# A gated mix of sliding attention and a mish MLP: order of issue planned from measured durations, exponentials listed later, two chunks per bank in the half products

## The chip, the cores and the metric

The kernel runs on one core of a Trainium2 chip. The metric is the device time of one execution in microseconds (us); lower is better. Engines are named as the profile names them: PE (TensorE, its matmuls; PEld its weight loads), DVE (VectorE), ACT (ScalarE), POOL (GpSimd) and SP (SyncE, which here only issues DMAs).

## The reference

The input x has 2048 rows of 640 numbers. Two branches are mixed row by row with a gate, all in f32:

```python
def a_branch(x, wqkv, wo):          # 32 heads of 20, window of 8 keys, 2 rows apart
    q, k, v = heads(x @ wqkv)       # wqkv 640 x 1920
    idx = pos[:, None] - 2 * arange(8)[None, :]
    logits = einsum("bhsd,bhswd->bhsw", q, k[idx]) * 20 ** -0.5
    logits = where(idx >= 0, logits, -1e9)
    o = einsum("bhsw,bhswd->bhsd", softmax(logits), v[idx])
    return o.reshape(2048, 640) @ wo

def b_branch(x, w1, b1, w2):        # w1 640 x 1728, w2 1728 x 640
    h = x @ w1 + b1
    return (h * tanh(softplus(h))) @ w2          # mish

g = sigmoid((x * gate_w).sum(-1, keepdims=True))
out = g * a_branch(x) + (1 - g) * b_branch(x)
```

## The kernel before

**Matmuls.** Every f32 matrix product is made of three products of rounded parts (`mm3`, L349): each operand is split into a high part (an ACT copy, L317) and a low part (a subtraction, L320), and PE does high x high (L352), high x low (L353) and low x high (L354), mostly on 128 x 128 weights and 512 columns. The low part is marked "ANY" in many places: it may run on DVE or on POOL, and the planner below decides which.

**Attention.** The columns of wqkv are cut into four groups of heads (hq) and the rows into two halves (P); that gives eight units. For a unit, PE makes q, k and v (`qkv`), ACT evacuates the banks (L489, L491, L493), and `attention` does the rest for eight groups of 128 rows, in two sets of four: scores (DVE product L397 and sum L400), a small mask for the first rows on POOL (`bounded`, L407), the softmax (DVE maximum L413, which waits for the mask, subtraction L414, ACT exponential L415), the shares (DVE L419 to L422), and the weighted values (DVE product L428 and adds L432, L433, L435), turned by a DVE transpose (L360) and put into DRAM.

**First MLP product.** `mlp1` makes one 128 x 512 block of h for one of 13 full chunks of the 1728 features (fc) and one of four sets of 512 rows (tb), 15 matmuls each; ACT applies mish (L593) and, for some, a negated copy (L596). The weight chunks W1[fc] are loaded through one single buffer, `raw1`, and split (128 x 640). The last 64 features (`mlp1_rest`) come out of the columns of x @ w1 that were computed beside qkv: a DVE transpose of `hx`, a round trip through DRAM (h), and a mish on 64 rows.

**Second MLP product.** The product with w2 is done with seven half products in place of eight (a Strassen-like scheme): `a, b, c, e, g, d, f`, each over KH = 7 chunks of 128 features, with four or six banks of PSUM (p, q, u, w, r, v) at once. Its operands are the blocks 11, 21, 22 and sums of blocks t1 to t4, all in DRAM. `put` writes a block with an SP DMA, and `plus` (L586) adds onto one with an accumulate DMA that POOL issues. t2 and t4 are made of others:

```python
done[at("t2")] = t2 + [plus(at("t2"), lambda: blk[at("t1")][low], t2 + done[at("t1")], rows=n)]
done[at("t4")] = done[at("t4")] + [plus(at("t4"), lambda: blk[at("t2")][low], done[at("t4")] + done[at("t2")], rows=n)]
```

so the second accumulate reads what the first has written in DRAM and has to wait until that has landed. In `mlp2` the first chunk and the last chunk of each half product are done bank by bank (three matmuls for each bank), the five between them in two parts, one for each half of the rows. `after_product` frees the banks: ACT copies (L771), and sums with `two` (L775) on DVE or "ANY". At the end `wo_out` multiplies the attention's output with wo, adds (L915) and stores.

**The order of issue.** Nothing is scheduled while the kernel runs: the class `Plan` decides it when the kernel is built. Each piece of work is added as a task with an engine, an assumed time in ns, a rank and the tasks that it follows. `Plan.run` then walks through an imagined execution: whenever an engine is free it takes, of the tasks that are ready and whose buffers are free, the one with the lowest rank and number, and the instruction is emitted at that moment. The order on each engine is therefore a result of the assumed times. An end is told to tasks on other engines LAG ns later ("done") and to tasks on the same engine through a second event ("own"). SP's DMAs share one imagined wire (`size / 270.0` ns each); a `plus` of 128 rows carries a size of 128 x 7000, so its imagined landing is some 3.3 us after its issue. Rings hold the buffers (8 banks, 7 `raw`, 3 `w`, 4 `hb`, one `raw1`); `ANY` work goes to DVE while DVE does scores only once it has been ready for PATIENCE = 2000 ns, and POOL keeps quiet beside the scores.

PE's own order is: a warm-up, qkv unit 0, then mlp1 chunks and qkv units in turn (mlp1 chunks 10, 11 and 12 for the first rows at about 274 to 285 us, and again for the other rows after the next units), the last two units up to about 394, the second MLP product up to about 575, and `wo_out`. The attention of a unit runs on DVE while PE is at later tasks.

Of the kernel before, what the change touches and what calls it, by code (L numbers as in the profile page):

```python
# [58 lines left out]
class Plan:  # L59
    PATIENCE = 2000  # L60
    LAG = {"PE": 220, "ACT": 120, "DVE": 120, "POOL": 150, "SP": 1900}
# [11 lines left out]
    def add(self, eng, ns, fn, after=(), rank=0.0, take=(), hold=(), size=0, kind=""):  # L73
# [12 lines left out]
        self.tasks.append(t)  # L86
        return t

    def run(self):
# [22 lines left out]
        while left:  # L112
            again = True
            while again:
                again = False
                for e in self.LAG:
# [52 lines left out]
            if what == "idle":  # L169
                busy[x] = False  # L170
                continue
# [21 lines left out]
def kernel(ctx: ExitStack, tc: tile.TileContext, x, wq, wo, w1, b1, w2, xt, gw, out):  # L193
# [42 lines left out]
    def act_ns(n):  # L236
        return 95 + 0.95 * n

    def dve_ns(n):
        return 150 + 1.05 * n  # L240
# [143 lines left out]
    def attention(u, P, hq, ready, gates):  # L384
# [10 lines left out]
        def scores(s0):  # L395
# [7 lines left out]
            step("DVE", 2830, red, rank=r, kind="qk sum")  # L403
# [6 lines left out]
        def softmax(a, after):  # L410

            h = slice(a, a + 4)
            step("DVE", 400, lambda: V.tensor_reduce(mx[:, h], lg[:, h], op=OP.max, axis=AX.X), [after], rank=r)  # L413
            step("DVE", 420, lambda: V.tensor_tensor(lg[:, h], lg[:, h], mx[:, h, :, None].to_broadcast([128, 4, HQ, W]), op=OP.subtract), rank=r)  # L414
            return step("ACT", 360 + 2 * TABLE, lambda: A.activation(lg[:, h], lg[:, h], AF.Exp, scale=scale), rank=-1)  # L415

        def shares(a, after):
            h = slice(a, a + 4)
            step("DVE", 400, lambda: V.tensor_reduce(sm[:, h], lg[:, h], op=OP.add, axis=AX.X), [after], rank=r)  # L419
            step("DVE", 330, lambda: V.reciprocal(sm[:, h], sm[:, h]), rank=r)  # L420
            step("DVE", 180, lambda: V.tensor_tensor(sm[:, h], sm[:, h], gate[:, P, h, None].to_broadcast([128, 4, HQ]), op=OP.mult), gates, rank=r)
            step("DVE", 640, lambda: V.tensor_tensor(pw[:, h].rearrange("p s w h -> p s h w"), lg[:, h], sm[:, h, :, None].to_broadcast([128, 4, HQ, W]), op=OP.mult), rank=r)  # L422

        def outputs(s0):
# [7 lines left out]
            step("DVE", 1510, lambda: V.tensor_tensor(pr[:, :, 0:4], pr[:, :, 0:4], pr[:, :, 4:8], op=OP.add), rank=r)  # L432
            step("DVE", 850, lambda: V.tensor_tensor(pr[:, :, 0:2], pr[:, :, 0:2], pr[:, :, 2:4], op=OP.add), rank=r)  # L433

            step("DVE", 515, lambda: V.tensor_tensor(q[:, s0:s0 + 2], pr[:, :, 0], pr[:, :, 1], op=OP.add), rank=r)  # L435

        def out(s0):
            ot = plan.buf("ot", lambda: at.tile([128, QF // 32, 4, 32], F32, name="ot"))
            step("DVE", 830, lambda: turn(ot.t, q[:, s0:s0 + 4], QF // 32), rank=r, take=[ot])
# [10 lines left out]
        e4 = softmax(4, fixed4)  # L450
# [3 lines left out]
        e0 = softmax(0, fixed0)  # L454
# [31 lines left out]
    def qkv_evac(u, P, hq, i, ps, done):  # L486
        kv, q, s = KV[UNIT[u]], Q[UNIT[u]], 4 * (1 - i // 4) + i % 4
        before = (freed.get((u - 2, s), []) + (dots if u == 1 else [])) if u < 7 else [zero2[0]]
        a = add("ACT", 400, lambda: A.activation(kv[:, 7 + s], ps.t[:, QF:3 * QF].rearrange("p (a b) -> p a b", a=2), AF.Copy),  # L489
                [done] + before, rank=SOON, hold=[ps])  # L490
        b = add("ACT", 280, lambda: A.activation(q[:, s], ps.t[:, :QF], AF.Copy), [a], rank=SOON, hold=[ps])  # L491

        c = add("ACT", 170, lambda: A.activation(hx[:, P, i, hq], ps.t[:, 3 * QF:3 * QF + RQ], AF.Copy), [b], rank=SOON, hold=[ps])  # L493
# [51 lines left out]
    def gate_dots(P):  # L545
# [6 lines left out]
        for s in range(8):  # L552
            i = 1 + s
            g = dma(lambda i=i: at(i), lambda s=s: xt[:, 2 * s + P], [dots[s]] if P else X[1, KC - 1].ready[:1], size=327680)
            done.append(add("DVE", 780, lambda i=i, s=s: V.tensor_tensor_reduce(
# [29 lines left out]
    def plus(key, src, after, hold=(), rows=128):  # L585
        return add("POOL", 1200, lambda: G.dma_start(out=blk[key][:rows], in_=src(), accum_op=OP.add, max_dma_last_dim=2048), after,  # L586
                   rank=-0.5, hold=hold, size=rows * 7000)

    def mish(src, n, fc, tb, after, hold):
# [3 lines left out]
        a = add("ACT", 610, lambda: A.activation(to(hb.t[:n]), src(), AF.Mish, bias=bias[:n, fc:fc + 1]),  # L593
                after + [bias_in], rank=NEXT, take=[hb], hold=hold)
        if half != h:
            a = add("ACT", 610, lambda: A.activation(hb.t[:n], hb.t[:n], AF.Copy, scale=-1.0), [a], rank=NEXT, hold=[hb])  # L596
# [158 lines left out]
    def mlp2(mid):  # L755
# [14 lines left out]
        def copy(to, of, after, take=()):  # L770
            return add("ACT", 610, lambda: A.activation(to.t, of.t, AF.Copy), after, rank=-0.5, take=take, hold=[to, of])  # L771
# [54 lines left out]

        for i, (k, kc) in enumerate(steps):
            name, of, names = PRODUCTS[k]
            while ahead < min(len(steps), i + 4):
                load_step(ahead)  # L830
                ahead += 1
            if i in mid:
                mid[i]()
            p, at, acts = loaded[i]
# [4 lines left out]
            if kc == KH - 1 and name in "agd":  # L839
                todo.sort(key=lambda x: (len(x[1]) == 1, x))  # L840
            parts = [[x] for x in todo] if kc in (0, KH - 1) else [todo[:len(names)], todo[len(names):]]
            for part in parts:
# [6 lines left out]
                first = {key: bank[key] in take for key in keys}  # L849
                stop = {key: kc == KH - 1 for key in keys}  # L850

                def run(part=part, keys=keys, p=p, at=at, acts=acts, first=first, stop=stop, names=names, name=name):
                    for (P, x), key in zip(part, keys):
                        c = at + names.index(x) * 128
                        mm3(bank[key].t, tuple(p.t[:, j, c:c + 128] for j in range(2)), tuple(acts[P].t[:, j] for j in range(2)),
                            first[key], stop[key], (key[0] + name) in ("pb", "qb", "wg", "rd", "vf"))

                Ps = sorted({P for P, _ in part})
                last = add("PE", 9 * len(part) / 3 * mm_ns(512), run,
                           [last] + p.ready + sum((acts[P].ready for P in Ps), []) + [read[key] for key in keys if key in read and kc == 0],  # L860
                           take=take, hold=[bank[key] for key in keys] + [p] + [acts[P] for P in Ps])
                if kc == KH - 1:
                    for key in keys:
                        ends[(name,) + key] = last
            if kc == KH - 1:
# [21 lines left out]
    def wo_out(tb):  # L887
# [13 lines left out]
        for dc in range(KC):  # L901
# [13 lines left out]
            v = add("DVE", 690, lambda b=b, ps=ps: V.tensor_tensor(as_slots(b.t), by_slot(ps.t), as_slots(b.t), op=OP.add),  # L915
# [116 lines left out]
```

## Time and profile before

| | |
|---|---|
| median of 3 runs | 650.08 us (648.77, 650.08, 650.43) |
| the profiled execution: time | 652.77 us |
| its span (first to last instruction) | 651.0 us |
| granted PE clock, mean | 0.992 |
| busy: PE, DVE, ACT, POOL | 637.3, 577.3, 264.4, 171.1 us |
| instructions: PE, DVE, ACT, POOL | 2805, 590, 557, 151 |
| DMA packets, bytes | 91324, 137.27 MB |

How to read it: the span is one execution, and the profiled time has 1.77 us around the span. Busy time is the sum over an engine's instructions; the forty slices of the profile show an engine's busy share in tenths (9 is 90% or more). In a timeline, a line has its start, its duration, engine, source line, operation, what it writes and reads, and in brackets how long the engine had been idle ahead of it and what ended that. "actt" are the blocks t1 to t4 in DRAM, "act" the others, "raw" and "hb" staging buffers, "pair" a split operand, "lg" the logits.

### The profile page before, as it was taken

To read this page: it belongs to the slowest core of one execution; us is meant where nothing else is said; L and a number is where in the kernel's file an instruction comes from. 1 tells how busy PE (TensorE), PEld (TensorE's weight loads), DVE (VectorE), ACT (ScalarE), POOL (GpSimd) and SP (SyncE) were. 2 spreads that over 40 slices of the span, in tenths; PEclk is the share of its full clock that TensorE was granted. 3 is DMA by queue.
4 is the path that set the end of the run, shared out by engine and by line. 5 is a ranking of instruction groups with operands and counts; after the bars stand their busy time and mean duration, and the time that the engine had idled before them with its cause. 6 is when DMAs were issued, how large, how long until landed. Compare 5 with 4: busy or idle time off the path is not lost.

```text
span 651.0 us, 8503 instructions
## 1 busy us (share of the span) xinstructions
PE 637.3 (98%) x2805; PEld 529.0 (81%) x2805; DVE 577.3 (89%) x590; ACT 264.4 (41%) x557; POOL 171.1 (26%) x151
## 2 busy tenths in 40 slices
PE   9999999999999999999999999779999999999997
PEld 6888888888888888888888888558888888888886
DVE  5769879999999989999998498899998999999862
ACT  6653552343235333333423314566756315831000
POOL 2021403821950220230233200561000254100630
PEclk9999999999999999999999999799999999999999
DMA  8999999776886983992799636977979239865352
GB/s 307 358 346 180 99 257 248 212 228 172 221 245 197 246 201 94 239 227 57 201 280 256 127 102 190 261 238 206 367 233 323 59 109 319 249 219 187 124 169 81
DMA packets 91324, 137.27 MB, mean 211 GB/s; under 512 B 12128, under 2 KB 41184, under 8 KB 91216
## 3 DMA queue, kind: packets, MB, share of 16 engines
q1 hardware_dynamic: 83600, 122.83, 61.2%
q0 software_dynamic: 7680, 13.90, 14.1%
q8 instruction: 22, 0.36, 0.2%
q14 instruction: 22, 0.18, 0.1%
HBM read 77.11 MB, written 57.81 MB: 207 GB/s over the span
## 4 chain that ended last, share of the span: by engine, by line
PE 90%; DVE 3%; DMA 3%; issue 1%; ACT 1%; SPq 1%; DVEq 0%; ACTq 0%
PE bank L352 30%; PE bank L354 30%; PE bank L353 30%; DVE pair L320 1%; PE bank L483 1%; DMA raw<-act 1%; DMA raw<-h 1%; DVE lg L400 1%; DMA h<-raw 1%; ACT pair L317 1%; PE bank L299 1%; SPq L326 1%; DMA hb<-in_w 0%; DVE pr L397 0%; DVE pr L432 0%
## 5 line engine op out<-in xcount | busy, mean ns | idle before, releaser
L352 PE MATMUL bank<-pair 128*128 128x512 f32 (+1 forms) x476 | 185.4, 390 | 4.7 <-ACT kvq L771 4.0
L353 PE MATMUL bank<-pair 128*128 128x512 f32 (+1 forms) x476 | 185.3, 389 | 4.1 <-POOL pair L320 4.1
L354 PE MATMUL bank<-pair 128*128 128x512 f32 (+1 forms) x476 | 185.0, 389 | 0.0
L352 PEld LDWEIGHTS bank<-pair 128*128 128x128 f32 x476 | 90.2, 190 | 23.2 <-ACT kvq L771 4.9
L353 PEld LDWEIGHTS bank<-pair 128*128 128x128 f32 x476 | 90.2, 190 | 21.8 <-POOL pair L320 4.4
L354 PEld LDWEIGHTS bank<-pair 128*128 128x128 f32 x476 | 90.2, 190 | 17.4
L317 ACT ACTIVATE pair<-raw 128x512 fp32r<-128x512 f32 (+3 forms) x122 | 72.8, 616 | 56.8 <-DMA raw<-o 27.2
L397 DVE TENSOR_TENSOR pr<-kvq 128x2560 f32<-128x2560 f32 x32 | 91.3, 2854 | 1.0 <-DMA kvq<-kvq 0.6
L400 DVE TENSOR_REDUCE lg<-pr 128x128 f32<-128x2560 f32 x32 | 90.2, 2820 | 1.0
L428 DVE TENSOR_TENSOR pr<-kvq,pw 128x2560 f32<-128x2560 f32 x32 | 90.3, 2822 | 0.7
L320 DVE TENSOR_TENSOR pair<-raw,pair 128x512 fp32r<-128x512 f32 (+3 forms) x109 | 71.1, 677 | 12.5 <-ACT pair L317 12.4
L593 ACT ACTIVATE hb<-bank,bias 128x512 f32<-128x512 f32 x52 | 35.9, 690 | 94.4 <-PE bank L354 91.6
L352 PE MATMUL bank<-pair,kvq 128*128 128x512 f32 (+1 forms) x188 | 72.6, 386 | 0.0
L354 PE MATMUL bank<-pair,kvq 128*128 128x512 f32 (+1 forms) x188 | 72.6, 386 | 0.0
L353 PE MATMUL bank<-pair,kvq 128*128 128x512 f32 (+1 forms) x188 | 72.6, 386 | 0.0
L352 PE MATMUL bank<-pair,w 128*128 128x512 f32 x182 | 70.8, 389 | 0.0
L353 PE MATMUL bank<-pair,w 128*128 128x512 f32 x182 | 70.8, 389 | 0.0
L354 PE MATMUL bank<-pair,w 128*128 128x512 f32 x182 | 70.8, 389 | 0.0
L586 POOL DMA_DIRECT2D actt<-hb x28 | 26.2, 957 | 165.1 <-ACT hb L593 74.5
L489 ACT ACTIVATE kvq<-bank 128x320 f32<-128x320 f32 x64 | 28.2, 441 | 72.7 <-PE bank L354 72.7
L317 ACT ACTIVATE pair<-hb 128x512 fp32r<-128x512 f32 (+3 forms) x63 | 38.8, 617 | 44.3 <-DMA hb<-o 22.1
L432 DVE TENSOR_TENSOR pr<-pr 128x1280 f32<-128x1280 f32 x32 | 48.0, 1499 | 0.7
(87 smaller groups left out, 841.4 us busy)
## 6 DMA issues: line engine op xcount, KB each, us to landing
actt<-hb SPq DMA_DIRECT2D x52, 256.0 KB, 5.3
act<-hb SPq DMA_DIRECT2D x38, 256.0 KB, 5.0
raw<-actt SPq DMA_DIRECT2D x32, 256.0 KB, 4.3
raw<-act SPq DMA_DIRECT2D x29, 256.0 KB, 4.4
actt<-hb POOLq DMA_DIRECT2D x26, 256.0 KB, 6.6
actt<-actt POOLq DMA_DIRECT2D x24, 256.0 KB, 6.8
hb<-actt SPq DMA_DIRECT2D x24, 256.0 KB, 4.6
kvq<-in_xt SPq DMA_DIRECT2D x16, 320.0 KB, 7.0
```

The source lines that it names most:

```text
L317: a = add("ACT", act_ns(n), lambda: A.activation(hi(), raw(), AF.Copy), after, rank=rank, take=take, hold=hold)
L320: return (V if e == "DVE" else G).tensor_tensor(lo(), raw(), hi().bitcast(F32), op=OP.subtract)
L352: nc.tensor.matmul(ps, ah, bh, start=first, stop=False, skip_group_check=more)
L353: nc.tensor.matmul(ps, ah, bl, start=False, stop=False, skip_group_check=more)
L354: nc.tensor.matmul(ps, al, bh, start=False, stop=last, skip_group_check=more)
L397: return V.tensor_tensor(pr, window(kv, s0, 0), q[:, s0:s0 + 2, None, :].to_broadcast([128, 2, W, QF]), op=OP.mult)
L400: V.tensor_reduce(lg_w[:, s0:s0 + 2], pr.rearrange("p s w (h d) -> p s w h d", d=DH), op=OP.add, axis=AX.X)
L428: V.tensor_tensor(pr.rearrange("p s w (h d) -> p s w h d", d=DH), vw, pw[:, s0:s0 + 2, :, :, None].to_broadcast([128, 2, W, HQ, DH]), op=O ...
L432: step("DVE", 1510, lambda: V.tensor_tensor(pr[:, :, 0:4], pr[:, :, 0:4], pr[:, :, 4:8], op=OP.add), rank=r)
L489: a = add("ACT", 400, lambda: A.activation(kv[:, 7 + s], ps.t[:, QF:3 * QF].rearrange("p (a b) -> p a b", a=2), AF.Copy), [done] + before, ...
L586: return add("POOL", 1200, lambda: G.dma_start(out=blk[key][:rows], in_=src(), accum_op=OP.add, max_dma_last_dim=2048), after, rank=-0.5, ...
L593: a = add("ACT", 610, lambda: A.activation(to(hb.t[:n]), src(), AF.Mish, bias=bias[:n, fc:fc + 1]), after + [bias_in], rank=NEXT, take=[hb ...
```

## The change

It edits the numbers and rules that the planner works with, and the order in which the second MLP product lists its tasks; what is computed stays the same.

- Assumed times: steps of DVE and ACT get other values (some 20 places), LAG is 220 for ACT and 200 for DVE (120 before), the wire is `size / 330`.
- Accumulate DMAs of POOL: they share SP's imagined wire and land 4000 ns (`ADDING`) after it; their size is rows x 4096.
- The "own" event: a task on the same engine is told at the end of the assumed issue, `now + t.ns`; before, 40 ns after the end with the landing in it.
- `late`: a task may be listed some time after it is ready; the exponentials of the second set are listed 1500 ns later, those of the first set 6000 ns later.
- Events of one time are all handled before anything is issued.
- `mlp2`: chunks 0 and 1, and chunks 5 and 6, are done together bank by bank (both chunks of one bank in a row, six matmuls), with the sorting of the banks and the loading ahead fitted to that.

```diff
-    LAG = {"PE": 220, "ACT": 120, "DVE": 120, "POOL": 150, "SP": 1900}
+    LAG = {"PE": 220, "ACT": 220, "DVE": 200, "POOL": 150, "SP": 1900}
+    ADDING = 4000
...
-        t = Task(eng, ns, fn, rank, size / 270.0)
-        t.kind = kind
+        t = Task(eng, ns, fn, rank, size / 330.0)
+        t.kind, t.late = kind, late
...
         while left:
-            again = True
+            again = not events or events[0][0] > now
...
                     end = now + t.ns
-                    if e == "SP":
+                    if t.land:
                         wire = max(wire, end) + t.land
-                        end = wire
-                    else:
-                        end += t.land
+                        end = wire + (0 if e == "SP" else self.ADDING)
                     heapq.heappush(events, (end + self.LAG[e], n + 1, "done", t))
                     if e != "SP":
-                        heapq.heappush(events, (end + 40, n + 2, "own", t))
+                        heapq.heappush(events, (now + t.ns, n + 2, "own", t))
...
                 if not t.waits:
                     t.why, t.rdy = x, now
-                    (shared if t.both else ready[t.eng]).append(t)
+                    heapq.heappush(events, (now + t.late, n, "ready", t))
+                    n += 1
...
     def act_ns(n):
-        return 95 + 0.95 * n
+        return 30 + 0.96 * n
     def dve_ns(n):
-        return 150 + 1.05 * n
+        return 75 + 1.03 * n
...
-        e4 = softmax(4, fixed4)
+        e4 = softmax(4, fixed4, 1500)
...
-        e0 = softmax(0, fixed0)
+        e0 = softmax(0, fixed0, 6000)
...
-                   rank=-0.5, hold=hold, size=rows * 7000)
+                   rank=-0.5, hold=hold, size=rows * 4096)
...
         for i, (k, kc) in enumerate(steps):
             name, of, names = PRODUCTS[k]
-            while ahead < min(len(steps), i + 4):
+            if kc in (1, KH - 1):
+                continue
+            kcs = [kc, kc + 1] if kc in (0, KH - 2) else [kc]
+            while ahead < min(len(steps), i + len(kcs) + 3):
...
-            if kc == KH - 1 and name in "agd":
+            if kc == KH - 2 and name in "agd":
                 todo.sort(key=lambda x: (len(x[1]) == 1, x))
-            parts = [[x] for x in todo] if kc in (0, KH - 1) else [todo[:len(names)], todo[len(names):]]
+            parts = [[x] for x in todo] if len(kcs) > 1 else [todo[:len(names)], todo[len(names):]]
             for part in parts:
...
+                for c in kcs:
+                    p, at, acts = loaded[i + c - kc]
+                    first = {key: bank[key] in take and c == kc for key in keys}
+                    stop = {key: c == KH - 1 for key in keys}
...
+                    last = add("PE", 9 * len(part) / 3 * mm_ns(512), run,
...
```

More of the change, by code (lines that the diff above doesn't have):

```diff
@@ L170, in run @@
                 busy[x] = False
+                continue
+            if what == "ready":
+                (shared if x.both else ready[x.eng]).append(x)
                 continue
@@ L402, in scores @@
             step("DVE", 2850, mul, ready[s0], rank=r, kind="qk")
-            step("DVE", 2830, red, rank=r, kind="qk sum")
+            step("DVE", 2750, red, rank=r, kind="qk sum")
         def bounded(a, b):
@@ L770, in copy @@
         def copy(to, of, after, take=()):
-            return add("ACT", 610, lambda: A.activation(to.t, of.t, AF.Copy), after, rank=-0.5, take=take, hold=[to, of])
+            return add("ACT", 540, lambda: A.activation(to.t, of.t, AF.Copy), after, rank=-0.5, take=take, hold=[to, of])
         def two(eng, out, a, b, op, after, take=(), rank=SOON):
@@ L848, in mlp2 @@
                         take.append(bank[key])
[L849 to L856, printed above, removed]
@@ L858, in mlp2 @@
-                Ps = sorted({P for P, _ in part})
[L859 to L865, printed above, removed]
+                Ps = sorted({P for P, _ in part})
@@ new lines, in mlp2, with run @@
+                for c in kcs:
+                    p, at, acts = loaded[i + c - kc]
+                    first = {key: bank[key] in take and c == kc for key in keys}
+                    stop = {key: c == KH - 1 for key in keys}
+                    def run(part=part, keys=keys, p=p, at=at, acts=acts, first=first, stop=stop, names=names, name=name):
+                        for (P, x), key in zip(part, keys):
+                            c = at + names.index(x) * 128
+                            mm3(bank[key].t, tuple(p.t[:, j, c:c + 128] for j in range(2)), tuple(acts[P].t[:, j] for j in range(2)),
+                                first[key], stop[key], (key[0] + name) in ("pb", "qb", "wg", "rd", "vf"))
+                    last = add("PE", 9 * len(part) / 3 * mm_ns(512), run,
+                               [last] + p.ready + sum((acts[P].ready for P in Ps), []) + [read[key] for key in keys if key in read and c == 0],
+                               take=take if c == kc else [], hold=[bank[key] for key in keys] + [p] + [acts[P] for P in Ps])
+                    if c == KH - 1:
+                        for key in keys:
+                            ends[(name,) + key] = last
@@ L866, in mlp2 @@
+            if kcs[-1] == KH - 1:
                 after_product(name)
```

47 lines of the change are left out of this document (24 added, 23 removed).

## The prediction

> **What bounds the kernel now.** I read the busy line first, then the forty slices, then the waits of TensorE (PE), then the timelines of the places that these name.
>
> ```profile
> PE 637.3 (98%) x2805; PEld 529.0 (81%) x2805; DVE 577.3 (89%) x590; ACT 264.4 (41%) x557; POOL 171.1 (26%) x151
> ...
> PE   9999999999999999999999999779999999999997
> ```
>
> PE is busy for 98% and its row of tenths dips in two neighbouring slices only, around 400 to 440 us. The wait list of PE agrees (line waited for: us in total, times, longest):
>
> ```profile
> PE bank L353 <- POOL pair L320: 4.1, 1, 4.1
> PE bank L352 <- ACT kvq L771: 4.0, 2, 3.8
> ...
> PE bank L352 <- ACT pair L317: 0.6, 1, 0.6
> ```
>
> PE's timeline there (start, duration, and in brackets the idle time before it and what ended that):
>
> ```profile
> 407.37 0.50 PE L352 MATMUL bank<-pair 128*128 128x512 f32 x1 [0.63 <-ACT pair L317]
> ...
> 411.97 0.79 PE L353 MATMUL bank<-pair 128*128 128x512 f32 x1 [4.10 <-POOL pair L320]
> ...
> 437.54 0.80 PE L352 MATMUL bank<-pair 128*128 128x512 f32 x1 [3.84 <-ACT kvq L771]
> ```
>
> Elsewhere a 512-column matmul starts every 0.227 us. From 406.35 to 416.70 there are 13 starts, which would take 2.95 us at that spacing and took 10.35: 7.4 lost, as 0.6 + 4.1 of waiting and 11 matmuls spaced 0.427 behind it (granted clock 0.83 in the window 400 to 420). From 432.17 to 440.58 there are 11 starts, 8.4 against 2.5: 5.9 lost (clock 0.93). So 13.3 us in all stand between this kernel and a gapless PE, which no listed change of order can beat, since the number of matmuls is unchanged.
>
> **Where the two pauses come from.** POOL:
>
> ```profile
> 353.68 0.87 POOL L586 DMA_DIRECT2D actt<-actt  x1 [3.66 <-DMA actt<-hb]
> 366.41 0.82 POOL L586 DMA_DIRECT2D actt<-actt  x1 [6.74 <-DMA actt<-actt]
> 366.95 0.64 POOL L407 TENSOR_TENSOR lg<-lg,bound 1x224 f32<-1x224 f32 x1
> ```
>
> DVE, and then ACT:
>
> ```profile
> 367.63 0.42 DVE L413 TENSOR_REDUCE mx<-lg 128x32 f32<-128x256 f32 x1 [9.45 <-POOL lg L407]
> ...
> 390.22 1.28 ACT L593 ACT_TABLE_LOAD   x1 [11.48 <-DMA raw<-h]
> 435.29 1.28 ACT L415 ACT_TABLE_LOAD   x1 [2.61 <-DVE lg L414]
> 436.91 1.07 ACT L771 ACTIVATE kvq<-bank 128x512 f32<-128x512 f32 x2
> ```
>
> An accumulate DMA on POOL that adds to the result of an earlier one waits until that has landed (6.74 us here), with the small mask (L407) queued behind it; DVE stands for 9.45 us for the mask; its late transpose (379.92) makes the last mish late on ACT (waits of 11.48 at 390.22 and 7.97 at 404.49), and POOL, waiting 36.0 us for that mish's block, does the low-part splits of the first product at 406.92 and 410.22 only. That is the first pause. The second is an ACT queue: an exponential waits 2.61 us for DVE and then loads its table (1.28), and the copies that free the banks stand behind it; 2.61 + 1.28 = 3.9 is about the 3.84 that PE waited.
>
> **The change, part by part.** *Second pause.* The exponentials are listed 1.5 and 6 us later, and in the new ACT order no exponential stands ahead of those copies. Doing two chunks of a bank in a row spaces the ends of banks by 6 matmuls (1.36 us) instead of 3 (0.68), over a copy of some 0.55. Matmul count and clock stay. I take all 5.9 off. The order has ten more table loads on ACT (10 x 1.28 = 12.8 us); ACT is busy for 41%, so they are hidden, if none stands ahead of an evacuation as the one at 435.29 did.
>
> *First pause.* In the new order POOL does five low splits of the first product ahead of the accumulate that waits for the last mish, where it did them behind. I take the 7.4 off.
>
> *What replaces them: the accumulate pairs.* The planner now counts a POOL accumulate as free to be followed by its dependent one as soon as it is issued. So in the new POOL order the two stand directly behind one another (before, other work stood between them), and POOL stands for the landing, whatever the planner assumes. From one issue to the dependent issue the trace shows 4.76 to 8.15 us, mean 6.8 over six pairs. Most such waits meet an idle POOL (26% busy). Three do not.
>
> (a) Low split of the last mlp1 weight chunk, W1[12]. Before:
>
> ```profile
> 274.25 1.69 POOL L586 DMA_DIRECT2D actt<-actt  x2 [4.38 <-DMA actt<-actt]
> 276.14 0.89 POOL L586 DMA_DIRECT2D actt<-hb  x1 [0.20 <-issue]
> 276.74 2.72 POOL L320 TENSOR_TENSOR w<-raw,w 128x640 fp32r<-128x640 f32 x1
> 282.95 0.84 POOL L586 DMA_DIRECT2D actt<-actt  x1 [3.49 <-DMA actt<-actt]
> ```
>
> PE first uses that low part in this matmul:
>
> ```profile
> 281.59 0.39 PE L354 MATMUL bank<-kvq,w 128*128 128x512 f32 x1
> ```
>
> It was ready 2.1 us early (276.74 + 2.72 = 279.46). In the new order it stands behind the dependent accumulate of block 0_2. From the same rows: dependent issue at 274.25, three entries of 0.54 to 0.64 behind it, first 0_2 accumulate at 276.0, landing 6.13 to 8.15 later (the pairs at 268.12 and 274.8), issue 0.55 to 0.6, split 1.56 (the same shape alone) to 2.72: ready at 284.2 to 287.5, a pause of 2.6 to 5.9, and some 1.8 of slow matmuls behind it (8 to 11 x 0.2 by the spacing above): 4.4 as the low end. High end: the mask of unit 3 is now queued behind two pairs too, so DVE would be some 4.5 late there; in the new SP order the puts of that unit's outputs stand ahead of the block that the pair adds to, and 0_2 starts 4.5 later: 5.9 + 4.5 + 2.2 = 12.6. No row tells the two apart, so I take the middle, 8.5, and keep both ends.
>
> The Trainium skill, "DMA: Bandwidth & Descriptors", section on the anatomy of one DMA on the SWDGE path, gives about 2.0 us plus bytes over 436 GB/s; my estimate from it for 256 KB is 2.6 us, and then this pause would be nil. The rows here (4.76 to 8.15) are for adding DMAs beside a busy SP queue, and differ.
>
> (b) Masks of attention unit 5: between its two masks now stand two whole pairs. The block that the first pair adds to had landed by 328.3 in the trace of before (an accumulate was released there), so: dependent issue 328.3 + 6.8 = 335.1, next pair 335.7 and 342.5, two entries more, mask at 343.7. Adding up DVE's instructions in the new order at their measured durations, I estimate that DVE wants it at 336 to 338: 6 to 8 late. DVE was busy 85.31 of 300 to 400, so idle for 14.69, of which 9.45 are the wait above; 5.2 are left to catch up in. 1 to 3 remains and meets the splits of the first product; I take 1. It could be 0, and at most the old 7.4.
>
> *(c) Work handed to POOL.* 28 elementwise operations move from DVE to POOL, mostly low splits. A DVE split starts 0.60 after the one before it when alone, so DVE saves 28 x 0.6 = 17 us. But DVE splits beside a POOL split took 1.49 to 1.65, +0.9 to 1.0, and POOL's 512-column split 1.29 alone and up to 3.7 beside a DVE product. If all 28 met a DVE operation it would lose 25. I take 1 us of late splits in the last products, where PE's own slack is small; 0 to 8 (25 - 17) is the bound.
>
> The Trainium skill, "SBUF — State Buffer", section on the two separate sides, has the port that VectorE and GpSimd share as an exclusive lock, the loser blocked. [...]
>
> The rest (measured spacings for assumed ones, 330 for 270 in SP's wire model, other lags) acts through the order alone, at nothing beyond the above; its cover is that PE's own order up to the first product is unchanged.
>
> **Sum.** The profiled execution took 652.77 (span 651.0 and 1.77 around it), 2.69 over the median of 650.08. 652.77 - 13.3 + 8.5 + 1 + 1 = 650.0; less 2.69, 647.3 us.
>
> **Rivals.**
> 1. *Clean*: accumulations land sooner (4.76 was seen), or POOL runs ahead, and W1[12] is in time. 652.77 - 13.3 - 2.69 = 636.8, or 638.8 with the two small terms. For it: POOL is idle much of the time. Against: 6.74, 5.14 and 4.38 of waiting in the rows above.
> 2. *DVE starved at the first product* (slower): the masks of unit 5 come 7 late and more than 5.2 of it stays, as in the row of 9.45; the last mish and the first splits are late again and 7.4 returns in the place of the 1: 653.7. It decides when that mask comes more than some 5.2 + 5 us after DVE wants it, or when the 5.2 of catching up isn't there. For it: two dependent accumulates instead of one. Against: splits no longer stand behind the last mish.
> 3. *POOL's new work makes DVE the bound in mlp2* (slower): DVE is at 96.05 of 100 in the window 460 to 560. More than 17/0.9 = 19 of the 28 must collide; at the bound +8 in the place of 1: 654.3.
> 4. *The change doesn't do what it says*: the order is not made from the trace's durations where it matters, since for dependent accumulates the landing of some 6.8 is left out of their order, and the old wait just moves along: both pauses shift, none is lost, near 650.
>
> **How the numbers follow.** Chances: forecast 0.45 (own range 643 to 651, 4.4 to 12.6 in the place of 8.5), clean 0.15, rival 2 0.20, rival 3 0.12, rival 4 0.08. The range 638 to 655 leaves out half of the clean case and the tails of 2 and 3. 0.3% (1.95 us) is about what a measurement here can tell from no change: faster is below 648.1, slower above 652.0. Faster: clean 0.15, some six tenths of the forecast 0.27, 0.05 of the others: 0.47. Same: 0.15 of the forecast, 0.05 of the fourth: 0.20. Slower: the rest, 0.33.
>
> **What would show it.** Right: no PE pause at 406 and 432; one new wait of PE near 281 on POOL's 640-column split, with a dependent accumulate's landing ahead of it on POOL. Wrong in the first step, if that wait is missing (then about 638) or the mask of unit 5 ends a DVE wait of over 6 us followed by a PE pause near 400; in the third, if PE waits for DVE splits in mlp2 in many small pieces. A time over 655 would mean a mechanism that is not listed here.

## The result, and the profile after

The changed kernel takes 686.96 us (median of 4 runs, 686.88 to 689.87) against 650.25 before: a ratio of 1.0578, 95% interval 1.0545 to 1.0612. The forecast was 647.3 with a range to 655. The profiled execution took 686.88 us, with a span of 685.1.

The busy line and PE's forty slices of the changed kernel:

```profile
PE 644.6 (94%) x2805; PEld 532.7 (78%) x2805; DVE 590.2 (86%) x562; ACT 272.5 (40%) x567; POOL 219.4 (32%) x179
...
PE   9999999999999999529999999699996999989997
```

The two slices below 9 inside the run have become five, and the deepest two lie at 274 to 308 us, where before had none. PE's waits (line waited for: us in total, times, longest; source lines have moved by 4 to 10, so L356 to L358 are the three matmuls, L324 the low split, L411 the mask, L775 the bank copies):

```profile
PE bank L358 <- POOL lg L411: 15.7, 1, 15.7
PE bank L358 <- POOL w L324: 6.3, 1, 6.3
PE bank L356 <- ACT kvq L775: 5.0, 1, 5.0
PE bank L356 <- ACT pair L321: 4.7, 2, 2.7
PE bank L357 <- DVE pair L324: 3.3, 3, 2.4
```

Below, "lost" is what the distances between matmul starts add up to beyond the full-rate 0.227 us, waiting and slow matmuls together. Before: 7.4 at 406 and 5.9 at 432, 13.3 in all. After: 26.2 at 277 to 308, 7.7 at 431, 0.5 and 8.4 at 517 to 537, 5.5 at 596: 48.3. The difference of 35.0 is the 34.1 by which the span grew, but for 0.9 less at the warm-up.

**The pause at 277 to 308** is W1 again, twice. POOL's timeline of the changed kernel:

```profile
279.86 0.89 POOL L590 DMA_DIRECT2D actt<-hb  x1 [21.14 <-DVE ot L364]
280.46 2.82 POOL L324 TENSOR_TENSOR w<-raw,w 128x640 fp32r<-128x640 f32 x1
285.86 0.85 POOL L590 DMA_DIRECT2D actt<-actt  x1 [2.58 <-DMA actt<-hb]
293.60 0.83 POOL L590 DMA_DIRECT2D actt<-actt  x1 [6.88 <-DMA actt<-actt]
...
301.50 0.83 POOL L590 DMA_DIRECT2D actt<-actt  x1 [5.19 <-DMA actt<-actt]
...
302.65 2.16 POOL L324 TENSOR_TENSOR w<-raw,w 128x640 fp32r<-128x640 f32 x1
```

The split at 280.46 is that of W1[11], the weight chunk before the last: it stands behind an accumulate that waited 21.14 us for a DVE transpose. That wait is the planner's "quiet" rule: a POOL instruction that is planned beside the scores is made to wait until DVE has come to them. PE needed the low part at 276.9 and stood 6.3. The split at 302.65 is that of W1[12]: six accumulates stand between the two splits, of which the first waited 2.58 for the block that it adds to, and two waited for landings, 6.88 and 5.19. PE stood 15.7 (put down to the mask behind the split in the list above). SP's timeline shows why the first of them came late:

```profile
279.20 1.29 SPq L330 DMA_DIRECT2D o<-ot  x3
...
281.03 0.45 SPq L330 DMA_DIRECT2D actt<-hb  x1
...
283.31 0.33 SPq L330 DMA_DIRECT2D raw<-in_w  x1
```

The block that the accumulate adds to is put at 281.03, behind stores of attention's output which wait for the same DVE transpose (278.33 to 279.17). The planner had that transpose at 258. In the kernel before it had it at 275, and the chip at 274.5. So on the chip the transpose comes 3.8 us later than before, but the plan runs 20 us ahead of it. The planner's own imagined execution ends at 636.6 us, against 644.2 for the kernel before.

**At the first product of the second MLP** (7.7 lost at 431) it is, as far as the rows show, the chain of the old first pause. The second mask of unit 5 ran on POOL at 376.19, behind two pairs of accumulates with waits of 7.80 and 7.96 for landings, and DVE stood for it longer than the 9.45 of before:

```profile
376.89 0.42 DVE L417 TENSOR_REDUCE mx<-lg 128x32 f32<-128x256 f32 x1 [12.05 <-POOL lg L411]
```

**Later in the second MLP product** an exponential with its table load is ahead of bank copies once more, at another boundary. ACT, changed kernel:

```profile
525.02 0.74 ACT L321 ACTIVATE kvq<-raw 128x640 fp32r<-128x640 f32 x1 [4.97 <-DMA raw<-in_wo]
...
528.68 1.28 ACT L419 ACT_TABLE_LOAD   x1
529.98 0.42 ACT L419 ACTIVATE lg<-lg 128x256 f32<-128x256 f32 x1
530.30 1.55 ACT L775 ACTIVATE kvq<-bank 128x512 f32<-128x512 f32 x3
```

PE waited 5.05 us for that copy, until 530.93. The exponential takes 1.7 us of it (528.68 to 530.40); ahead of it ACT had stood 4.97 us for a load of wo, with seven splits queued behind that. Which of the two counts was not tried. The kernel before has waits of ACT of up to 6.70 us for wo that cost PE nothing.

### The profile page after: what moved, and what is told of

Its sections match the earlier page's. It is cut to its first block, busy times and chain, and to the rows that moved or that the text cites. A ratio compares the mean times of both kernels' runs of the same rounds, so it can differ in the third digit from the quotient of the medians.

```text
span 685.1 us, 8515 instructions
## 1 busy us (share of the span) xinstructions
PE 644.6 (94%) x2805; PEld 532.7 (78%) x2805; DVE 590.2 (86%) x562; ACT 272.5 (40%) x567; POOL 219.4 (32%) x179
## 3 DMA queue, kind: packets, MB, share of 16 engines
q0 software_dynamic: 7680, 13.90, 13.3%
## 4 chain that ended last, share of the span: by engine, by line
PE 20%; DVE 19%; DMA 11%; issue 7%; POOL 4%; ACT 2%; SPq 1%; DVEq 0%; POOLq 0%; ACTq 0%
PE bank L358 7%; PE bank L357 7%; PE bank L356 7%; DVE pair L324 4%; DVE pr L432 4%; DMA actt<-actt 3%; DMA raw<-actt 2%; DVE pr L436 2%; DVE pr L401 2%; DVE lg L404 2%; DVE pr L437 1%; ACT pair L321 1%; POOL pair L324 1%; DMA hb<-actt 1%; POOL actt L590 1%
## 5 line engine op out<-in xcount | busy, mean ns | idle before, releaser
L356 PE MATMUL bank<-pair 128*128 128x512 f32 (+1 forms) x476 | 186.7, 392 | 9.7 <-ACT kvq L775 5.0
L358 PE MATMUL bank<-pair 128*128 128x512 f32 (+1 forms) x476 | 186.0, 391 | 0.0
L356 PEld LDWEIGHTS bank<-pair 128*128 128x128 f32 x476 | 90.9, 191 | 28.8 <-ACT pair L321 5.9
L358 PEld LDWEIGHTS bank<-pair 128*128 128x128 f32 x476 | 90.9, 191 | 17.5
L401 DVE TENSOR_TENSOR pr<-kvq 128x2560 f32<-128x2560 f32 x32 | 92.7, 2898 | 7.4 <-ACT kvq L493 3.7
L321 ACT ACTIVATE pair<-raw 128x512 fp32r<-128x512 f32 (+3 forms) x122 | 71.3, 615 | 45.2 <-DMA raw<-s 17.2
L324 DVE TENSOR_TENSOR pair<-raw,pair 128x512 fp32r<-128x512 f32 (+3 forms) x95 | 74.1, 804 | 4.2 <-ACT pair L321 4.1
L358 PE MATMUL bank<-pair,kvq 128*128 128x512 f32 (+1 forms) x188 | 72.6, 386 | 0.0
L356 PE MATMUL bank<-pair,kvq 128*128 128x512 f32 (+1 forms) x188 | 72.5, 386 | 0.0
L356 PE MATMUL bank<-pair,w 128*128 128x512 f32 x182 | 70.8, 389 | 0.0
L358 PE MATMUL bank<-pair,w 128*128 128x512 f32 x182 | 70.8, 389 | 0.0
L324 POOL TENSOR_TENSOR pair<-raw,pair 128x512 fp32r<-128x512 f32 (+2 forms) x27 | 47.4, 1783 | 36.1 <-ACT pair L321 27.2
L590 POOL DMA_DIRECT2D actt<-actt x28 | 25.4, 937 | 94.7 <-DMA actt<-actt 75.9
L358 PE MATMUL bank<-kvq,w 128*128 128x512 f32 x78 | 32.4, 415 | 22.0 <-POOL lg L411 15.7
```

The source lines that it names most:

```text
L321: a = add("ACT", act_ns(n), lambda: A.activation(hi(), raw(), AF.Copy), after, rank=rank, take=take, hold=hold)
L324: return (V if e == "DVE" else G).tensor_tensor(lo(), raw(), hi().bitcast(F32), op=OP.subtract)
L356: nc.tensor.matmul(ps, ah, bh, start=first, stop=False, skip_group_check=more)
L358: nc.tensor.matmul(ps, al, bh, start=False, stop=last, skip_group_check=more)
L401: return V.tensor_tensor(pr, window(kv, s0, 0), q[:, s0:s0 + 2, None, :].to_broadcast([128, 2, W, QF]), op=OP.mult)
```

## The experiments

Two theories. **A**: the accumulate pairs, as the prediction has them: POOL stands for a landing with urgent work behind it. **B**: the clock of the plan: imagined times that run ahead of the chip's DVE put things in an order in which PE's operands stand behind entries that wait for DVE. All times are beside 650.0 to 651.4 for the kernel before on the same chip. e12 is the median of five executions, e14 to e16 of four; the others are one execution each.

| run | us | lost by PE, where |
|---|---|---|
| e1 landing counted | 665.8 | 15.1 at 280; 8.1 at 507; 3.2 at 579 |
| e2 no quiet wait | 700.6 | 29.6 at 280; 2.7 and 11.3 at 428 to 453; 9.8 at 531; 7.4 at 608 |
| e3 old clock | 685.0 | 13.5 at 229; 19.4 at 421; 12.3 in smaller ones |
| e4 moves alone | 646.05 | 5.1 at 407; 1.3 at 624 |
| e5 pairs alone | 668.8 | 10.0 at 281; 7.1 at 406; 7.0 at 424; 5.1 at 449 |
| e6 clock alone | 695.7 | 22.6 at 281; 7.3 at 429; 12.1 at 551; 13.3 at 598 |
| e7 both back | 660.3 | 11.7 at 228; 7.2 at 418; 1.7 at 500 |
| e8 banks alone | 648.65 | 6.1 at 406; 3.0 at 545 to 565 |
| e9 wire alone | 666.3 | 20.4 at 278; 5.7 at 427 to 452 |
| e10 times alone | 663.3 | 10.5 at 113; 13.3 at 463 to 582 |
| e11 ADDING alone | 678.7 | 21.5 at 226; 4.5 at 427; 6.3 at 482 to 501; 7.4 at 588 |
| e12 landing longer, with moves | 640.2 | 2.2 at 617 |
| e13 stores later | 666.6 | 13.2 at 281; 7.6 at 498 to 515; 6.2 at 576 |
| e14 landing longer alone | 645.1 | 4.8 at 425 |
| e15 landing and banks | 642.6 | 0.8 at 429; 3.1 at 540 to 560 |
| e16 moves alone, timed | 646.7 | 5.5 at 406; 1.6 at 624 |

### One rule of the change put back (e1, e2, e3, e7)

e1, on the changed kernel:

```diff
-    heapq.heappush(events, (now + t.ns, n + 2, "own", t))
+    heapq.heappush(events, (end + 40 if t.land else now + t.ns, n + 2, "own", t))
```

> The changed kernel with one rule put back: for an accumulate DMA of POOL the event for the next task on POOL comes after the imagined landing again; all else as changed. The order that comes out keeps DVE's imagined times; on POOL other work stands again between the two accumulates of a pair, and the low split of W1[12] no longer stands behind two dependent accumulates. Theory A (accumulate pairs, as in the prediction): both pauses near 277 and 289 (26.7 us with their slow matmuls) come from the pairs, so both go: about 660. Theory B (the plan's clock runs ahead of the chip: DVE is 15 to 20 us later on the chip than in the plan, and in-order queues of POOL and SP hold W1 behind entries that wait for DVE): the pause near 277 stays, since no pair stands ahead of that split, and the one near 289 shrinks from 16 to about 6, because the blocks still leave late behind SP's stores: 675 to 679.

21 us came back, between the two. The pause at 277 went (B had it stay), and 11.2 us of waiting for W1[12]'s split stayed (A had it go): its split stood behind a mask that waited for DVE's sums (282.63 to 285.79) and the accumulates behind that, and then took 3.89 itself.

e2: the same order on every engine, `follow` does nothing.

```diff
     def follow(ins, gate):
-        tc.add_manual_dep(ins.ins, gate.ins.name, ...)
+        pass
```

> The changed kernel with the same order on every engine, without the extra waits that hold a POOL instruction issued beside the scores until DVE has reached them (they carry no data). Theory A: they have no part in it, no change: 685 to 688. Theory B: the waits of 18.2 and 21.1 us on POOL for DVE's transpose are these waits; without them the low split of W1[11] runs before 277 and the pause of 6.4 + 2.4 there goes. W1[12] is still loaded at about 283, since its load stands on SP behind stores that wait for DVE, and its split still stands behind two landings: that pause grows by about what the first one gave back. So the first pause gone and the time still 680 to 687. If POOL also runs further ahead with its accumulates, the second shrinks too, to no less than about 6: 668.

W1[11]'s split ran at 265.37 and the pause at 277 was gone, as B said; but the load of W1[12] still stood on SP behind the stores until 286.74 (DVE now 4.7 later), so PE waited 10.5 for the high part and 16.1 for the low part. Slower, not equal: 29.6 lost near 280 in place of 26.2. The extra wait was a symptom, and taking it away alone does not help. The other 31 us lost in this run were not traced.

e3: the wire, the assumed times and LAG of before, on the changed kernel.

```diff
-    LAG = {"PE": 220, "ACT": 220, "DVE": 200, "POOL": 150, "SP": 1900}
+    LAG = {"PE": 220, "ACT": 120, "DVE": 120, "POOL": 150, "SP": 1900}
-        t = Task(eng, ns, fn, rank, size / 330.0)
+        t = Task(eng, ns, fn, rank, size / 270.0)
-        return 75 + 1.03 * n
+        return 150 + 1.05 * n
... and the other assumed times
```

> The changed kernel with the assumed times, LAG and the wire of 270 of the kernel before; the event without landing, ADDING, the late exponentials and the bank-by-bank order stay. DVE's imagined times come within some 5 us of where the chip had DVE in both traces up to 260 us. Theory A: the pairs are still one behind the other, so pauses near 280 stay: over 665. Theory B: most of the time comes back: the pauses near 280 shrink to under 5 together, 650 to 662 with what is left in mlp2.

In time hardly anything came back, over 665 as A had it. But the pauses near 280 went, as B had it: 1.3 is left, at 295. So neither theory held as it stands. W1[12]'s low split had moved from POOL to DVE (295.67, in 0.82 us), where no pair stands ahead of it, so this run doesn't tell what the pairs would have done there. The time was lost at two other places. At 229 PE waited for splits of qkv weights, 4.8 in two waits for DVE and 5.1 for POOL, there behind a landing of 6.42. At 421 it was the mask of unit 5 again, the second rival's chain, on DVE:

```profile
369.73 0.42 DVE L417 TENSOR_REDUCE mx<-lg 128x32 f32<-128x256 f32 x1 [11.19 <-POOL lg L411]
```

e7: both e1's and e3's edits.

> The changed kernel with both put back: landings counted and the old assumed times, LAG and wire. What stays of the change: ADDING, the late exponentials, 40 ns less between neighbours on one engine, chunks bank by bank. If A and B are the two causes, little is left near 280 (under 4 us) and in mlp2: 645 to 655. If another part has a share (ADDING, the missing 40 ns), over 658.

Nothing is lost near 280: the clock put back takes that pause away, with the pairs (e3) or without, and counting the landings alone takes 11 us off it (e1). But the time is over 658, so another part has a share: 11.7 were lost at 228, where e3 lost 13.5 and where ADDING alone (e11) has its pause. The planner itself has PE idle there in its imagined execution, for 7.6 us up to 235 in e3 and e7.

### One part of the change alone, on the kernel before (e4, e5, e6, e8, e9, e10, e11)

e5 is the cleanest: only the event of POOL's accumulates, DVE's planned times unchanged.

```diff
-    heapq.heappush(events, (end + 40, n + 2, "own", t))
+    heapq.heappush(events, (now + t.ns if t.land else end + 40, n + 2, "own", t))
```

> The kernel before with one rule of the change alone: a POOL accumulate tells the next task on POOL at the end of its issue, the landing not counted. DVE's imagined times are those of the kernel before to the microsecond; the two accumulates of a pair now stand one behind the other on POOL, and the low split of W1[12] stands behind two pairs. Theory A (the pairs): two landings of 6 to 8 us from 268 on put that split at 283 to 286 against 281.6, a pause of 2 to 4 with 1.8 of slow matmuls near 281, and masks of attention come late, so that the pause near 410 stays or grows: 655 to 664. Theory B (the clock of the plan): its clock is that of the kernel before, so 649 to 652.

POOL in that run, then PE:

```profile
276.01 0.82 POOL L586 DMA_DIRECT2D actt<-actt  x1 [6.38 <-DMA actt<-actt]
...
286.38 0.82 POOL L586 DMA_DIRECT2D actt<-actt  x1 [7.75 <-DMA actt<-actt]
...
287.50 2.17 POOL L320 TENSOR_TENSOR w<-raw,w 128x640 fp32r<-128x640 f32 x1
```

```profile
289.73 0.80 PE L354 MATMUL bank<-kvq,w 128*128 128x512 f32 x1 [7.93 <-POOL w L320]
```

Two landings, then the split: 7.9 of waiting, where 2 to 4 was expected, and 2.1 of slow matmuls. That is A, shown alone; the time was 5 above what was expected, also since the later pauses grew by 5.9 in sum.

e6: assumed times, LAG and the wire of 330, the edits of e3 the other way round. e10: the same without the wire. e9: the wire alone, which is

```diff
-        t = Task(eng, ns, fn, rank, size / 270.0)
+        t = Task(eng, ns, fn, rank, size / 330.0)
```

> The kernel before with the assumed times, the LAG and the wire of 330 of the change alone: DVE's imagined times run 10 to 12 us ahead of the places where the chip had DVE up to 260 us, and landings are counted as before. Theory A: POOL's order has no new pairs, so no pause near 280, and the time is within 4 us of the kernel before. Theory B: SP's and POOL's entries are tied to a DVE that is late, so pauses near 280 or in the first product of at least 8 us: 658 or more.

> The kernel before with the wire of 330 for 270 alone. DVE's imagined times come out 9 us earlier from unit 0 on (84 for 93 us at the first turned output, where the chip had 92 to 96), since the loads of the first 100 us are imagined quicker than the 257 to 264 GB/s that the chip moved there. Together with the assumed times it cost 45 us (pauses of 22.6 near 281, 12.1 near 551, 13.3 near 600). Theory B by way of the wire: most of the pause near 281 is here, 10 us or more, 658 to 675. If the assumed times make it, within 4 us of the kernel before.

> The kernel before with the assumed times and the LAG of the change alone, the wire at 270. DVE's imagined times run 6 us early at 87 us and 9 to 14 us early at 250 to 320. Theory B by way of the times: pauses near 281 and, since shorter DVE times and cheaper splits hand more work to POOL, in mlp2: 658 or more, of which the two late pauses of the run with both (25 us). If the wire makes it, within 4 us of the kernel before near 281; the late ones tell the split of work.

e6 cost 45 us, the most of all; landings were counted in it, at the planner's 3.3 us, so this is B without the edit of A. It isn't without waits for landings: 6.21 and 5.38 of them stand ahead of the split below. e9 cost 16 with 20.4 lost near 280, as B has it: from 78 us of the plan on, DVE ran 11 us behind it, and 20 at 241. e10 cost 13, but DVE stayed within 5 us of its plan to 380 us and nothing of note was lost near 280: 10.5 went at 113, where PE waited for low splits of the qkv weights (the planner has PE idle there too, for 7.6 us), and 13.3 in mlp2, where POOL has 25 instructions more than before over the whole run (176 and 151). So the wire made the clock run ahead; the shorter times did other harm, of which only the place is known. POOL in e6:

```profile
279.33 0.84 POOL L586 DMA_DIRECT2D actt<-actt  x1 [16.44 <-DVE ot L360]
...
287.30 0.84 POOL L586 DMA_DIRECT2D actt<-actt  x1 [6.21 <-DMA actt<-actt]
...
298.68 0.84 POOL L586 DMA_DIRECT2D actt<-actt  x1 [5.38 <-DMA actt<-actt]
...
299.74 1.52 POOL L320 TENSOR_TENSOR w<-raw,w 128x640 fp32r<-128x640 f32 x1
```

e11: ADDING, the shared wire and rows x 4096 alone.

```diff
-                    if e == "SP":
+                    if t.land:
                         wire = max(wire, end) + t.land
-                        end = wire
-                    else:
-                        end += t.land
+                        end = wire + (0 if e == "SP" else self.ADDING)
...
-                   rank=-0.5, hold=hold, size=rows * 7000)
+                   rank=-0.5, hold=hold, size=rows * 4096)
```

> The kernel before with the accumulate DMAs on SP's imagined wire and ADDING alone: an accumulate of 128 rows is imagined to land 4000 ns and its turn on the wire after its issue (some 6 us, near the measured 6.8, for 3.3 before), and the next task on POOL is told only then. This is theory A turned round: POOL should stand less. If right: the mask of unit 5 comes earlier, the pause near 410 falls from 7.4 to under 3, the one near 435 stays: 643 to 648. If the order that it gives has other faults (more work handed to POOL in mlp2), 650 or more.

The opposite of what was hoped: 28 us slower. SP issued the loads of a unit's qkv weights at 180 to 189 us before, here at 217 to 238, for matmuls from 226 on:

```profile
217.45 3.47 SPq L325 DMA_DIRECT2D raw<-in_wq  x3
...
235.31 2.71 SPq L325 DMA_DIRECT2D raw<-in_wq  x4
```

The `raw` buffers that they use were with the sums of w2, which POOL finished at 222 in place of 182.5. Why the planner moved those was not tried. But it is neither A nor B: from 60 us on DVE stayed within 4.5 us of the plan, and the planner's own imagined execution has PE idle there, for 20.8 us up to 248.7.

e4 (later exponentials and banks), e8 (banks alone) and e16 (e4 timed):

```diff
-        e0 = softmax(0, fixed0)
+        e0 = softmax(0, fixed0, 6000)          # e4, e16; 1500 for the exponential e4
...
+            kcs = [kc, kc + 1] if kc in (0, KH - 2) else [kc]      # e4, e8, e16, as in the change
```

> The kernel before with two parts of the change alone: the exponentials listed 1500 and 6000 ns later, and chunks 0, 1 and 5, 6 of each half product bank by bank. Up to 390 us the imagined times are those of the kernel before. Theory A and B both: no pause near 280. If these two moves were what takes the second pause away, the 5.9 us near 435 go, and the 7.4 us near 410 stay: 644. If the pause near 435 only moves with DVE being 10 us late there, 650 or more.

> The kernel before with chunks 0, 1 and 5, 6 of each half product bank by bank, and the exponentials as before. The run with both moves had no pause near 435. If the bank order is what took it away, 645 to 647; if it is the later exponentials, the pause near 435 stays and the time is 649 to 652.

> The kernel of the run of 646.05 again (later exponentials and bank order alone), timed: 644 to 647 if that look was typical.

The pause at 432 went in all three, so the bank order takes it away; e8 ends between its two expectations, because 3.0 of small waits came in. e16 has a ratio of 0.9941 (0.9919 to 0.9963). So the later exponentials and the bank order together are a small gain; the loss is in the planner's numbers and rules.

### What ties W1 to the late DVE (e13)

```diff
-            spilled[tb, hq] = turned_out(..., lambda: ot.t, [prev], [ot])
+            spilled[tb, hq] = turned_out(..., lambda: ot.t, [prev], [ot], 8000)   # passed on as late
```

> The changed kernel with landings counted (as in the run of 665.77, which has one pause of 15.1 us from 280 to 298) and the stores of attention's outputs listed 8 us after they are ready, so that on SP the load of W1[12] and the blocks of mish stand ahead of the stores that wait for DVE; DVE's imagined times are the same within 2 us. If SP's queue is what ties W1 to the late DVE: that pause falls to under 5, 650 to 657. If POOL's entries (mask and extra wait) are the tie: it stays at 11 to 16, 662 to 668.

It stayed: SP now had the load ahead of the stores, and POOL's mask still waited until 282.12, when DVE's sum (279.14 + 2.82) was done. With landings counted the tie is POOL's own queue; in e2 it was SP's too.

### The landing made longer (e12, e14, e15)

```diff
-                   rank=-0.5, hold=hold, size=rows * 7000)
+                   rank=-0.5, hold=hold, size=rows * 15000)
```

> The kernel before with the late exponentials and the bank-by-bank order, as in the run of 646.05, and the imagined landing of an accumulate DMA at 7.1 us for 3.3 (measured mean 6.8), with the next task on POOL told after it. On POOL one chained accumulate moves behind the mask of unit 5, so that the mask no longer waits for its 6.7 us. Theory A: the mask, the last mish and the splits of the first product come earlier, the pause of 5.1 near 410 falls to under 2: 641 to 644. If the splits there are late for another reason: 645 to 647.

> The kernel before with the imagined landing of an accumulate DMA at 7.1 for 3.3 us alone. The mask of unit 5 no longer stands behind the last chained accumulate. Theory A: the pause of 7.4 near 410 goes, wholly or but for 2; the pause of 5.9 near 435, an exponential ahead of copies, stays or goes with DVE being 8 us earlier: 638 to 645.

> The kernel before with the longer imagined landing and the bank-by-bank order, the exponentials as before. If the later exponentials have a part of their own: 642 to 645, with a pause in mlp2 that 640.2 did not have. If not: 639.5 to 641.

The edit is all of e14; e15 adds the bank order, e12 the bank order and the later exponentials. On the kernel before, this one number is A turned round: 128 x 15000 / 270 is 7.1 us, against the measured 6.8. Alone it is worth 0.9913 (0.9893 to 0.9932), and the pause at 406 is gone. With the bank order 0.9867 (0.9840 to 0.9894), with the later exponentials as well 0.9838 (0.9815 to 0.9860): 640.2 us, better than both kernels and just below its expectation. Page and POOL of e12:

```profile
PE 631.9 (99%) x2805; PEld 525.7 (82%) x2805; DVE 579.3 (91%) x595; ACT 265.3 (42%) x559; POOL 183.0 (29%) x146
```

```profile
357.16 0.82 POOL L590 DMA_DIRECT2D actt<-actt  x1 [1.92 <-DVE lg L404]
357.70 0.69 POOL L411 TENSOR_TENSOR lg<-lg,bound 1x224 f32<-1x224 f32 x1
```

The mask of unit 5 ran at 357.70, where it ran at 366.95 before: the chained accumulate that held it is now behind it. PE lost 2.2 in one place. The intervals of e12 and e15 overlap, so a part of the later exponentials beside these two is likely (e15 has the pause in mlp2 that was expected for that case, 3.1 at 540 to 560) but not shown.

## Why the prediction was wrong

- *What bounds the kernel*: right. 13.3 us were to be had, and e12 got nearly all of them by order alone: its span is 638.5, and 651.0 - 13.3 = 637.7.
- *Term (a), pairs ahead of W1[12]*: the mechanism was right, and alone (e5) it cost 10.0 where 8.5 was forecast. In the whole change 26.2 were lost there, over the high end of 12.6. The length of the walk was right: from the first accumulate to the end of the split it has 16.1 to 19.4 us (268.12 to 284.2 or 287.5), and the changed kernel took 18.95 (285.86 to 304.81). Its start was wrong: it was taken from the trace of before, and it came 17.7 us later, behind the put at 281.03. And W1[11] was not looked at: the quiet wait ahead of it was in the source, and was left out of the waits that the working listed.
- *"The rest acts through the order alone, at nothing beyond the above"*: this is the step that failed. The wire cost 16 us alone, times and LAG 13, both together 45, ADDING 28, and putting the wire, the times and LAG back took the loss near 280 from 26.2 to 1.3 (e3, where other losses took its place). Its cover, that PE's order stays the same, was no cover: PE stands for operands whose order on POOL and SP did change. These costs don't add up (the whole is 37).
- *High walk of (a)*: it had DVE 4.5 us late, and on the chip the transpose came 3.8 later than before. But it let only the second pair wait for that; in the changed order the first pair waits too. The order was made for a DVE 20 us earlier than the chip's. The prediction compared orders, and never the planner's clock with the trace; before, the two agreed within 3 us from 48 to 340 us.
- *First pause, -7.4*: didn't go. Moved by the 26 us lost earlier it is the one at 431, with 7.7; POOL's splits do come earlier, and now the high splits on ACT stand behind the last mish (430.90, after a wait of 4.52 for its load), which is late as before. *Second pause, -5.9*: gone at its place by the bank order, as e8 shows, but 8.4 are lost at a later boundary, where an exponential is ahead of copies, the condition that the prediction itself had named, and a wait of ACT for wo ahead of both.
- *Term (b)*, 1 us: its own sign of being wrong is in the changed kernel. DVE stood 12.05 us for the mask of unit 5, where the working had it 6 to 8 late, and PE lost 7.7 at 431. So rival 2 came true there, at about its price of 7.4. In e3, with the pairs and the old clock, DVE stood 11.19 us for that mask and PE lost 19.4 in the first product, where the price is too small. *Term (c)*, 1 us: mlp2 lost 14.4 in all; how much of it is the 28 operations on POOL was not measured apart.
- *The chance*: slower had 0.33 with no mechanism above 655, since each rival was priced at one place; that a time over 655 would mean an unlisted mechanism was said, and is so. Rival 4 (the order isn't made from the trace's durations where it matters) named half of the cause, the landing, and put its price at nothing. No rival has the plan's clock.

The estimate of 2.6 us for a landing, which the prediction worked out from the Trainium skill ("DMA: Bandwidth & Descriptors", anatomy of one DMA on the SWDGE path), would have made the pause of term (a) nil. The changed kernel waited 6.88 and 5.19 us for landings there, e5 6.38 and 7.75, and a plan with 7.1 is the fastest of those here.

## What to carry to other kernels

Where the order is made from assumed times, compare the planner's clock with the trace, engine by engine, before and after: a padded number may be what keeps them together, and a smaller one may pull them apart (the wire at 270, where the trace moved 257 to 264 GB/s, and at 330). Look too whether the planner's own imagined execution already has the bottleneck idle: in e3, e7, e10 and e11 it had. An in-order queue that waits for a landing has to be planned with that landing, for what is behind it too; one such number (e14, 5 us) was worth more here than the two other gains together (e16, 3 us). Where a change is a bundle, try its parts one by one: here the bank order and the later exponentials were a gain, and each of the planner's new numbers and rules that was tried alone (e5, e9, e10, e11) a loss. The 40 ns less between neighbours were not tried alone.

## What was not expected of the hardware

- The mask, one row of 168 numbers, takes 0.54 us on POOL in four of the eight units of the kernel before, but 3.15 in e13 where it starts as a DVE product does (282.12 on POOL, the product at 282.06 for 2.83): the mask ended 0.38 us after the product. The Trainium skill ("SBUF — State Buffer", the two separate sides) has the port that the two share as an exclusive lock; this row agrees.
- The slow matmuls behind a pause don't grow with it: in the changed kernel PE ran 7 of them spaced 0.38 to 0.43 us after 15.7 us of waiting (305.45 to 308.4), 9 after 6.3 us, and 13 after 5.05 us.
